# Chunk 0's first product in units of 128 tokens by four column blocks, in an attention kernel followed by a gated two-layer product

## The chip, the cores and the metric

The kernel runs on one core of a Trainium2 chip. The metric is the device time of one execution in microseconds (us). The core has a matrix engine (TensorE, PE in the profile, with its weight loads shown apart as PEld), a vector engine (VectorE, DVE), a scalar engine (ScalarE, ACT), GpSimd (POOL) and SyncE (SP). Each works through its own queue in the order in which the program issues instructions to it; semaphores hold an instruction until its inputs are there. POOL and SP also issue DMA transfers.

## The reference

```python
# q, k, v: 8 batches, 8 heads, 576 positions, 64 wide
def phi(x, c, s):                       # c, s: cosine and sine of the position
    r = np.maximum(x, 0.0)
    return np.concatenate([r * c, r * s], axis=-1)
q_p = phi(q, cos_w, sin_w); k_p = phi(k, cos_w, sin_w)
kv  = np.einsum('bhsf,bhsd->bhfd', k_p, v)
z   = np.sum(k_p, axis=2)
x   = (q_p @ kv) / (q_p @ z + 1e-6)     # per head; heads joined: 4608 tokens x 512
h   = x @ w_in                          # 512 -> 2048
g   = h * np.cos(h)
out = g @ w_out                         # 2048 -> 512
```

## The kernel before, in words

The 4608 tokens are cut into nine chunks of 512 for the two products, and into eight batches of 576 for the attention. Attention for a batch has these steps, each a small function:

- `load_q`, `load_kv`, `load_rest`: DMA loads on POOL's queue, from float32 to float16. A batch's q is kept as six parts of 96 rows.
- `scaled(b, which, i)`: one part of q or k through the map phi, two instructions (cosine and sine half), on VectorE (L143), a few of batch 0 on ScalarE (L138).
- `q_turn(b, i)`: eight TensorE transpositions of a scaled part of q (L167) into PSUM, and a copy to the tile X. For batches from 2 on, a DMA transposition on SP's queue does this.
- `spread_v`: v is copied into a tile vz, in which each row of 64 is followed by ones, so that one matmul gives kv and z. Batch 0 has no vz; there an access pattern takes 64 ones from the end of v's own tile, and the matmuls are 128 columns wide (L219) rather than 65 (L209).
- `kv_head(b, h)`: five accumulating matmuls for one head, and a copy of four heads to the tile kvz (L224).
- `num_tile(b, t)`: for a tile of 128 tokens, eight matmuls give numerator and denominator (L235), VectorE adds 1e-6 (dn, L242), takes the reciprocal (rd, L246) and multiplies (x, L255).
- `x_turn(b, t)`: four TensorE transpositions of x (L273) and a copy into XT (L281 on ScalarE, L279 on VectorE), the input of the first product.

The first product of a chunk, `m1_group`, takes one block of 128 columns of w_in at a time: four matmuls of 512 tokens (L288), the cosine on ScalarE (co, L294), the product g on VectorE (L297). Chunk 0 is done in two halves of 256 tokens, so that it can begin when two x tiles are there: 32 steps. The second product, `m2_part`, accumulates sixteen matmuls (L307) for each 128 tokens, ScalarE copies the result (ost, L314), and SP's queue stores it.

The order of everything is written out by hand (`tc.manual_schedule()`): `plan_stage0`, `plan_ahead` and `plan_tiles` put steps of attention into a table under (chunk, step) with `at(c, s, f, ...)`, and `run(c, s)` issues what stands there right behind step s of the products. Batch 0's attention comes ahead of the products and among chunk 0's first product, batch 1's among chunk 0's second product. `warm(n)` issues n matmuls on zeros.

PSUM has two pools: psA (tag att, two buffers) for attention, and psM (tags m1 and m2, two buffers each) for the products and some early attention tiles.

Of the kernel before, what the change touches and what calls it, by code (L numbers as in the profile page):

```python
# [11 lines left out]
ALU = mybir.AluOpType  # L12
# [5 lines left out]
def kernel(  # L18
# [14 lines left out]
    R = 6  # L33
# [39 lines left out]
    KB = [cpool.tile([PK, H * RUNK], F16, name=f"k{n}") for n in "ab"]  # L73
    VB = [cpool.tile([PK, H * RUNK + D], F16, name=f"v{n}") for n in "ab"]
    ID = cpool.tile([P, P], F16, name="ID")
# [72 lines left out]

    def q_turn(b, i, tag="m1"):
        s = st[b]  # L150
        if i == 0:
            s["X"] = apool.tile([P, H, S], F16, name="X", tag="X")
        if b >= 2:
            nc.sync.dma_start_transpose(
                out=s["X"][:, :, i * PR:(i + 1) * PR], in_=s["qp"][:, i],
            )
            return
        if b == 1:
            if i % 2 == 0:
                s["QT"] = psA.tile([P, 2, H, P], F16, name="QT", tag="att")  # L160
            QT = s["QT"][:, i % 2]
        elif i >= 4:
            QT = psA.tile([P, 2, H, P], F16, name="QT", tag="att")[:, 0]
        else:
            QT = psM.tile([P, H, P], F16, name="QT", tag=tag)
        for h in range(H):
            nc.tensor.matmul(  # L167
                QT[:, h, 0:PR], lhsT=s["qp"][:, i, h * F:(h + 1) * F], rhs=ID[0:PR, 0:PR],
                is_transpose=True,
            )  # L170
        if b == 1 and i % 2 == 0:
            return
        i0 = i - (b == 1)
        dst = s["X"][:, :, i0 * PR:(i + 1) * PR]
        if b == 1 and i > 1:
            nc.vector.tensor_copy(
                out=dst.rearrange("p h (a c) -> p a h c", a=2),
                in_=s["QT"][:, :, :, 0:PR],
            )
        elif b == 1:  # L180
            nc.scalar.activation(
                out=dst.rearrange("p h (a c) -> p a h c", a=2),
                in_=s["QT"][:, :, :, 0:PR], func=AF.Copy,
            )
        else:
            nc.scalar.activation(out=dst, in_=QT[:, :, 0:PR], func=AF.Copy)

    def spread_v(b, h):
        s = st[b]
        if h == 0:  # L190
            s["vz"] = apool.tile([PK, H, RK, VS], F16, name="vz", tag="vz", bufs=1)
            nc.gpsimd.memset(s["vz"][:, :, :, D:VS], 1.0)
        src = s["v16"][:, 0:H * RUNK].rearrange("p (h i d) -> p h i d", i=RK, d=D)
        dst = s["vz"][:, h:h + 2, :, 0:D]
        if b != 2:
            nc.scalar.activation(out=dst, in_=src[:, h:h + 2], func=AF.Copy)  # L196
        else:
            nc.vector.tensor_copy(out=dst, in_=src[:, h:h + 2])

    def kv_head(b, h):  # L200
        s = st[b]
        if h == 0 or (b == 0 and h == 4):
            s["KV"] = psA.tile([P, H, P], F32, name="KV", tag="att")
        if h == 0:
            s["kvz"] = apool.tile([P, H, D + 1], F16, name="kvz", tag="kvz")
        n = P if b == 0 else D + 1
        for i in range(RK):
            if b > 0:
                nc.tensor.matmul(  # L209
                    s["KV"][:, h, 0:n], lhsT=s["kp"][:, i, h * F:(h + 1) * F],  # L210
                    rhs=s["vz"][:, h, i, 0:n], start=(i == 0), stop=(i == RK - 1),
                )
                continue
            base = s["v16"][:, h * RUNK + i * D: h * RUNK + (i + 1) * D]
            vz = bass.AP(
                tensor=base.tensor, offset=base.offset,
                ap=[list(base.ap[0]), [H * RUNK - h * RUNK - i * D, 2], [1, D]],
            )
            nc.tensor.matmul(  # L219
                s["KV"][:, h], lhsT=s["kp"][:, i, h * F:(h + 1) * F], rhs=vz,  # L220
                start=(i == 0), stop=(i == RK - 1),
            )
        if h % 4 == 3:
            nc.scalar.activation(  # L224
                out=s["kvz"][:, h - 3:h + 1], in_=s["KV"][:, h - 3:h + 1, 0:D + 1],
                func=AF.Copy,
            )

    def num_tile(b, t, whole=True):
# [30 lines left out]
    def x_turn(b, t):  # L260
# [3 lines left out]
        if b >= 2:  # L264
            nc.sync.dma_start_transpose(out=XT[:, :, n0:n0 + new], in_=x[P - new:P, :])
            return
        if b == 0 and t < 2:
            XPf = psM.tile([P, 1024], F16, name="XP", tag="m1")
        else:
            XPf = psA.tile([P, 2048], F16, name="XP", tag="att")  # L270
        XP = XPf[:, 0:NCT * P].rearrange("p (i c) -> p i c", c=P)
# [10 lines left out]

    def m1_group(c, j, n0=0, n1=CH):
        if ("g", c) not in st:
            st["g", c] = gpool.tile([P, NJT, CH], F16, name="g", tag="g")
        M1 = psM.tile([P, CH], F32, name="M1", tag=("m1", "m2")[j % 2])
        for i in range(NCT):
            nc.tensor.matmul(  # L288
                M1[:, n0:n1], lhsT=w_in_sb[:, i, j * P:(j + 1) * P],
                rhs=XT[:, i, c * CH + n0:c * CH + n1],  # L290
                start=(i == 0), stop=(i == NCT - 1),
            )
        co = opool.tile([P, CH], F32, name="co", tag="co")
        nc.scalar.activation(  # L294
            out=co[:, n0:n1], in_=M1[:, n0:n1], func=AF.Sin, bias=PIH, scale=1.0,
        )
        nc.vector.tensor_tensor(  # L297
            out=st["g", c][:, j, n0:n1], in0=M1[:, n0:n1], in1=co[:, n0:n1], op=ALU.mult,
        )
# [27 lines left out]
    def at(c, s, f, *args):  # L327
        plan.setdefault((c, s), []).append((f, args))

    HS = NJT  # L330
    M2S = NJT
# [10 lines left out]
    def plan_stage0():  # L342
        at(0, 1, q_turn, 0, 4)
        at(0, 2, scaled, 0, "q", 5)
        at(0, 3, x_turn, 0, 2)
        at(0, 4, loads, 2, "kvq")
        at(0, 6, q_turn, 0, 5)
        for t, n in ((3, 9), (4, HS + 6)):
            at(0, n, num_tile, 0, t, False)
            at(0, n + 1, normalise, 0, t, 0, 1)  # L350
            at(0, n + 2, normalise, 0, t, 1, 2)
            at(0, n + 5, x_turn, 0, t)
        z = 2 * HS
        for i in range(R):
# [3 lines left out]
        for n in range(4):  # L358
            at(0, z + 1 + n, spread_v, 1, 2 * n)
        for h in range(4):  # L360
            at(0, z + 4, kv_head, 1, h)
        for i in range(2):
            at(0, z + 5, q_turn, 1, i)
        for h in range(4, H):
            at(0, z + 5, kv_head, 1, h)
        for i in range(2, R):
            at(0, z + 5 + i // 2, q_turn, 1, i)
        for n, f, t in ((7, num_tile, 0), (8, num_tile, 1), (9, x_turn, 0),
                        (10, num_tile, 2), (10, x_turn, 1), (12, num_tile, 3),
                        (13, x_turn, 2), (14, x_turn, 3), (14, num_tile, 4)):  # L370
            at(0, z + n, f, 1, t)
        at(1, 2, x_turn, 1, 4)
        for i, n in enumerate((9, 10, 11, 12, 13)):
            at(0, z + n, scaled, 2, "k", i)
        for n in range(4):
            at(0, z + 12 + n, spread_v, 2, 2 * n)
        for i, n in enumerate((-1, 1, 2, 4, 6, 8)):
# [39 lines left out]
    with tc.manual_schedule():  # L417
# [9 lines left out]
        nc.scalar.activation(out=WS, in_=PIH, func=AF.Sin)  # L427
        tiles_for(0)
        load_kv(0, "k", 0, 4)
        load_rest(0, "k")  # L430
        load_kv(0, "k", 4, 8)
        load_q(0, 0, 4)
        for h in range(0, H, 2):
            if h == 2:
                load_rest(0, "v")
            load_kv(0, "v", h, h + 2)
        nc.gpsimd.memset(st[0]["v16"][:, H * RUNK:], 1.0)
        load_w_in(0)
        load_q(0, 4, R)
        for g in range(1, 4):  # L440
# [11 lines left out]

        warm(33)
        for h0 in (0, 4):
            for i in range(RK):
                scaled(0, "k", i, h0, h0 + 4)
        for i in range(4):
            scaled(0, "q", i)
            if i < 2:
                q_turn(0, i)  # L460
        for h in range(8):
            kv_head(0, h)
        q_turn(0, 2, "m2")
        num_tile(0, 0)
        q_turn(0, 3)
        warm(1)
        num_tile(0, 1)
        warm(3)
        x_turn(0, 0)
        warm(2)  # L470
        scaled(0, "q", 4)
        x_turn(0, 1)
        num_tile(0, 2)
        for s in range(2 * HS):
            n = s // HS * (CH // 2)
            m1_group(0, s % HS, n, n + CH // 2)
            run(0, s)
        order = [(m, g) for p in (0, 2) for g in range(2) for m in (p, p + 1)]
        order += [(m, g) for m in range(NSUB) for g in range(2, 4)]
        for s, (m, g) in enumerate(order):  # L480
            m2_part(0, m, g)
            run(0, 2 * HS + s)
        for c in range(1, NCHUNK):
# [37 lines left out]
```

## Time and profile before

| | us |
|---|---|
| median of 3 runs (lowest, highest) | 300.72 (299.48, 300.94) |
| the profiled execution's own time | 299.56 |
| its span, first to last instruction | 297.8 |
| TensorE matmuls busy | 290.4 (98%) |
| VectorE busy | 190.3 (64%) |
| ScalarE busy | 158.7 (53%) |
| first matmul of the first product (L288) | 19.19 |
| first matmul of the second product (L307) that runs on without a stop | 36.71 |
| chunk 1's first product | 56.35 |

The first three rows are times of executions. The busy times are sums over one profiled execution, and the last three rows are moments in it, counted from the start of the span. A matmul's busy time is modelled and overlaps that of the next, so a high share doesn't say that TensorE never waited; the chain that ended last and the stages do.

### The profile page before, as it was taken

The numbers are of one execution on the slowest core, as the hardware profiler recorded it, in microseconds if no ns is written. First come the engines' busy times: TensorE is split into PE (matmuls) and PEld (weight loads), VectorE is DVE, ScalarE is ACT, GpSimd is POOL, SyncE is SP. The second block draws the span as 40 slices with busy tenths as digits, with TensorE's granted clock in tenths as the row PEclk, the third lists the DMA queues.
The fourth block names the chain that finished last, engine by engine and source line by source line (L and its number), as shares of the span: only waits on it lengthen the run. The fifth ranks groups of instructions, "written<-read, shape, count | busy, mean of one in ns | idle before, by whom it ended". The sixth has DMA issues, their size and how long they took to land.

```text
span 297.8 us, 5456 instructions
## 1 busy us (share of the span) xinstructions
PE 290.4 (98%) x2031; PEld 150.9 (51%) x2031; DVE 190.3 (64%) x470; ACT 158.7 (53%) x261; POOL 39.8 (13%) x65
## 2 busy tenths in 40 slices
PE   8999999999999999999999999999999999999994
PEld 3577756554544544455445544554455444444441
DVE  1668987988489666966686768677766267007600
ACT  1589952676357624762477158715771177137511
POOL 8733310005004002100210022000000000000000
PEclk9999999999999999999999999999999999999999
DMA  6999999589999996996799959996702610121022
GB/s 89 181 203 206 200 206 200 155 108 134 188 170 147 179 186 117 199 168 130 123 165 181 149 116 169 161 163 136 163 16 70 118 35 0 41 76 28 0 73 70
DMA packets 78019, 38.84 MB, mean 130 GB/s; under 512 B 48296, under 2 KB 73384, under 8 KB 77992
## 3 DMA queue, kind: packets, MB, share of 16 engines
q0 software_dynamic: 28240, 18.36, 44.1%
q1 hardware_dynamic: 49752, 20.13, 38.6%
q8 instruction: 16, 0.26, 0.4%
q14 instruction: 11, 0.09, 0.1%
HBM read 36.76 MB, written 9.44 MB: 155 GB/s over the span
## 4 chain that ended last, share of the span: by engine, by line
PE 89%; DVE 5%; DMA 3%; ACT 1%; POOL 1%; issue 1%; ACTq 0%; POOLq 0%
PE M L307 42%; PE M L288 38%; PE NP L235 3%; DVE g L297 3%; PE KV L209 3%; DMA q<-in_q_dram 3%; PE QT L167 1%; ACT co L294 1%; PE KV L219 1%; PE XP L273 1%; DVE qp L143 1%; POOL ka L108 1%; DVE x L255 0%; PE W L451 0%; POOL ka L115 0%
## 5 line engine op out<-in xcount | busy, mean ns | idle before, releaser
L297 DVE TENSOR_TENSOR g<-M,co 128x512 f16<-128x512 f32 (+1 forms) x160 | 99.9, 635 | 57.5 <-ACT co L294 57.4
L307 PE MATMUL M<-w_out_sb,g 128*128 128x512 f16 x576 | 132.3, 379 | 0.1
L288 PE MATMUL M<-XT,w_in_sb 128*128 128x512 f16 (+1 forms) x640 | 129.5, 358 | 0.6 <-DVE dn L242 0.3
L294 ACT ACTIVATE co<-M,PIH 128x512 f32<-128x512 f32 (+1 forms) x160 | 101.9, 647 | 27.5 <-PE M L288 27.0
L288 PEld LDWEIGHTS <-w_in_sb 128*128 128x128 f16 x640 | 61.3, 98 | 59.7 <-issue 0.9
L307 PEld LDWEIGHTS <-g 128*128 128x128 f16 x576 | 53.8, 98 | 58.7 <-issue 0.3
L314 ACT ACTIVATE ost<-M 128x512 f32<-128x512 f32 x36 | 21.5, 597 | 93.4 <-PE M L307 68.4
L255 DVE TENSOR_TENSOR x<-NP,rd 128x512 f16<-128x512 f32 (+1 forms) x42 | 27.9, 664 | 4.9 <-DMA XT<-x 3.6
L143 DVE TENSOR_SCALAR qp<-q,CS 96x512 f16<-96x512 f16 x94 | 28.5, 350 | 2.1 <-DMA q<-in_q_dram 1.2
L143 DVE TENSOR_SCALAR kp<-ka,CS 116x512 f16<-116x512 f16 (+1 forms) x75 | 21.6, 345 | 5.4 <-DMA ka<-in_k_dram 5.4
L235 PEld LDWEIGHTS <-X 128*128 128x128 f16 x320 | 15.3, 98 | 8.7 <-issue 0.8
L100 POOL DMA_DIRECT2D q<-in_q_dram x9 | 7.0, 779 | 90.8 <-DVE qp L143 88.2
L235 PE MATMUL NP<-kvz,X 128*128 128x65 f16 x320 | 17.0, 194 | 0.2 <-issue 0.2
L242 DVE TENSOR_SCALAR dn<-NP 128x8 f32<-128x8 f32 x40 | 6.5, 162 | 15.4 <-PE NP L235 15.2
L196 ACT ACTIVATE vz<-va 116x640 f16<-116x640 f16 x20 | 13.5, 727 | 0.0
L451 PE MATMUL W<-WU 128*128 128x512 f16 x39 | 12.0, 470 | 1.2 <-DVE PIH L426 1.2
L209 PEld LDWEIGHTS <-kp 116*128 116x128 f16 x280 | 10.7, 98 | 3.1
L209 PE MATMUL KV<-vz,kp 116*128 116x65 f16 x280 | 11.2, 193 | 0.0
L246 DVE RECIPROCAL rd<-dn 128x8 f32<-128x8 f32 x40 | 8.1, 203 | 1.4
L108 POOL DMA_DIRECT2D ka<-in_k_dram x8 | 6.5, 817 | 18.3 <-DVE kp L143 14.9
L451 PEld LDWEIGHTS <-WU 128*128 128x128 f16 x39 | 4.4, 117 | 7.2 <-issue 3.9
L224 ACT ACTIVATE kvz<-KV 128x260 f16<-128x260 f32 x16 | 6.2, 387 | 3.3 <-PE KV L209 2.3
(35 smaller groups left out, 74.5 us busy)
## 6 DMA issues: line engine op xcount, KB each, us to landing
out_dram<-ost SPq DMA_DIRECT2D x24, 192.0 KB, 2.3
q<-in_q_dram POOLq DMA_DIRECT2D x7, 576.0 KB, 7.6
ka<-in_k_dram POOLq DMA_DIRECT2D x6, 560.0 KB, 13.2
va<-in_v_dram POOLq DMA_DIRECT2D x6, 560.0 KB, 11.8
out_dram<-ost SPq DMA_DIRECT2D x24, 128.0 KB, 5.9
w_in_sb<-in_moe_w_in_dram POOLq DMA_DIRECT2D x4, 512.0 KB, 9.9
w_out_sb<-in_moe_w_out_dram POOLq DMA_DIRECT2D x4, 512.0 KB, 16.7
out_dram<-ost SPq DMA_DIRECT2D x24, 64.0 KB, 3.1
```

Source lines behind the costliest of these rows:

```text
L108: nc.gpsimd.dma_start(out=rows_of(st[b][which + "16"])[0:FULL, h0:h1], in_=full[:, h0:h1],)
L143: nc.vector.tensor_scalar(out=dst[:, h0:h1, t, :], in0=src[:, h0:h1, i, :], scalar1=0.0, scalar2=cs[:, t], op0=ALU.max, op1=ALU.mult,)
L196: nc.scalar.activation(out=dst, in_=src[:, h:h + 2], func=AF.Copy)
L209: nc.tensor.matmul(s["KV"][:, h, 0:n], lhsT=s["kp"][:, i, h * F:(h + 1) * F], rhs=s["vz"][:, h, i, 0:n], start=(i == 0), stop=(i == RK - 1),)
L235: nc.tensor.matmul(NP[:, h // 4, o:o + D + 1], lhsT=s["X"][:, h, c0:c0 + P], rhs=s["kvz"][:, h], start=True, stop=True,)
L255: nc.vector.tensor_tensor(out=x4[:, a0:a1], in0=np4[:, a0:a1, :, 0:D], in1=rd[:, a0:a1].broadcast_to((P, a1 - a0, 4, D)), op=ALU.mult,)
L288: nc.tensor.matmul(M1[:, n0:n1], lhsT=w_in_sb[:, i, j * P:(j + 1) * P], rhs=XT[:, i, c * CH + n0:c * CH + n1], start=(i == 0), stop=(i == ...
L294: nc.scalar.activation(out=co[:, n0:n1], in_=M1[:, n0:n1], func=AF.Sin, bias=PIH, scale=1.0,)
L297: nc.vector.tensor_tensor(out=st["g", c][:, j, n0:n1], in0=M1[:, n0:n1], in1=co[:, n0:n1], op=ALU.mult,)
L307: nc.tensor.matmul(M2, lhsT=st["g", c][:, j, m * P:(m + 1) * P], rhs=w_out_sb[:, j], start=(j == 0), stop=(j == NJT - 1),)
L314: nc.scalar.activation(out=ost, in_=M2, func=AF.Copy)
L451: nc.tensor.matmul(W, lhsT=WU[:, 0:P], rhs=WU, start=True, stop=True)
```

## The change

- Chunk 0's first product is done by `m1_unit(u, k_, t)`: 128 tokens (tile t) by four column blocks (group k_), 16 matmuls of 128 columns into one PSUM buffer, then one cosine and one product g of 128x512. There are 16 units, in the order written in `units`. x tile 1 is turned inside unit 0.
- Batch 0 gets a vz tile as the others have; VectorE sets the ones and spreads v in four pieces. Its matmuls are 65 columns wide. Heads 4 to 7 are copied to kvz in twos.
- The first x tile of batch 0 is made in two halves of four heads (`first_half`), each turned by itself (`first_turn`).
- The first load of q brings three parts in place of four, the second the other three. The parts 1 and 3 of batch 0 are copied to X by VectorE.
- Part 3 of q, and x tiles 2 and 3, are placed among the units; parts 3, 4 and 5 are each turned right behind their scaling. Batch 1's heads, turns and x tiles stand later in chunk 0's second product, and its v is spread by both engines.

Lines of the diff that the steps speak of:

```diff
-    def q_turn(b, i, tag="m1"):
+    def q_turn(b, i, tag="m1", evict=True):
...
-        elif i >= 4:
+        elif i >= 3:
             QT = psA.tile([P, 2, H, P], F16, name="QT", tag="att")[:, 0]
...
+    def q_evict(b, i):
...
+        if b == 0 and i in (1, 3):
+            nc.vector.tensor_copy(out=dst, in_=QT[:, :, 0:PR])
...
-        if b != 2:
+        if b > 2 or b == 1 and h < 4:
             nc.scalar.activation(out=dst, in_=src[:, h:h + 2], func=AF.Copy)
         else:
             nc.vector.tensor_copy(out=dst, in_=src[:, h:h + 2])
...
+    def first_half(a):
+        s = st[0]
+        NP = psM.tile([P, 4, P], F32, name="NP", tag="m1")
+        for h in range(4):
+            nc.tensor.matmul(
+                NP[:, h, 0:D + 1], lhsT=s["X"][:, 4 * a + h, 0:P], rhs=s["kvz"][:, 4 * a + h],
+                start=True, stop=True,
+            )
...
+    def m1_unit(u, k_, t):
+        M1 = psM.tile([P, 4, P], F32, name="M1", tag=("m1", "m2")[u % 2])
+        for j in range(4):
+            for i in range(NCT):
+                f0 = (4 * k_ + j) * P
+                nc.tensor.matmul(
+                    M1[:, j], lhsT=w_in_sb[:, i, f0:f0 + P],
+                    rhs=XT[:, i, t * P:(t + 1) * P],
+                    start=(i == 0), stop=(i == NCT - 1),
+                )
+        if u == 0:
+            x_turn(0, 1)
+        co = opool.tile([P, 4, P], F32, name="co", tag="co")
+        nc.scalar.activation(out=co, in_=M1, func=AF.Sin, bias=PIH, scale=1.0)
+        nc.vector.tensor_tensor(
+            out=g_for(0)[:, 4 * k_:4 * k_ + 4, t * P:(t + 1) * P], in0=M1, in1=co,
+            op=ALU.mult,
+        )
...
     def plan_stage0():
-        at(0, 1, q_turn, 0, 4)
+        for i in (3, 4):
+            at(0, 1, scaled, 0, "q", i)
+            at(0, 1, q_turn, 0, i)
+        at(0, 1, num_tile, 0, 2)
         at(0, 2, scaled, 0, "q", 5)
+        at(0, 2, q_turn, 0, 5)
         at(0, 3, x_turn, 0, 2)
+        at(0, 3, num_tile, 0, 3)
         at(0, 4, loads, 2, "kvq")
-        at(0, 6, q_turn, 0, 5)
-        for t, n in ((3, 9), (4, HS + 6)):
...
+        at(0, 5, x_turn, 0, 3)
+        at(0, 9, num_tile, 0, 4, False)
...
-        for n, f, t in ((7, num_tile, 0), (8, num_tile, 1), (9, x_turn, 0),
-                        (10, num_tile, 2), (10, x_turn, 1), (12, num_tile, 3),
-                        (13, x_turn, 2), (14, x_turn, 3), (14, num_tile, 4)):
+        for n, f, t in ((9, num_tile, 0), (10, num_tile, 1), (11, x_turn, 0),
+                        (12, num_tile, 2), (12, x_turn, 1), (13, num_tile, 3),
+                        (14, x_turn, 2), (14, num_tile, 4), (15, x_turn, 3)):
...
+        ones_for(0, nc.vector)
...
-        load_q(0, 0, 4)
+        load_q(0, 0, 3)
...
-        nc.gpsimd.memset(st[0]["v16"][:, H * RUNK:], 1.0)
         load_w_in(0)
-        load_q(0, 4, R)
+        load_q(0, 3, R)
...
-        warm(33)
+        warm(31)
...
-        for i in range(4):
+        for i in range(2):
             scaled(0, "q", i)
-            if i < 2:
-                q_turn(0, i)
-        for h in range(8):
+            q_turn(0, i, evict=(i == 0))
+        for h in range(H):
+            if h == 4:
+                q_evict(0, 1)
+                scaled(0, "q", 2)
+                q_turn(0, 2, "m2", evict=False)
+            if h % 2 == 0:
+                spread_v(0, h)
+            if h == 6:
+                first_half(0)
             kv_head(0, h)
-        q_turn(0, 2, "m2")
...
+        q_evict(0, 2)
+        first_turn(0)
+        first_half(1)
+        warm(2)
+        first_turn(1)
         num_tile(0, 1)
...
-        for s in range(2 * HS):
-            n = s // HS * (CH // 2)
-            m1_group(0, s % HS, n, n + CH // 2)
+        units = [(0, 0), (0, 1), (1, 0), (1, 1), (0, 2), (1, 2), (0, 3), (1, 3)]
+        units += [(g, t) for g in (2, 3) for t in range(NSUB)]
+        for s, (g, t) in enumerate(units):
+            m1_unit(s, g, t)
             run(0, s)
```

## The prediction

> **What bounds the kernel now.** I read the page first, then busy time by stage, then the chain that ended last, then the timeline of the first 40 us. All times are us of the profiled execution, from the span's start.
>
> ```profile
> PE 290.4 (98%) x2031; PEld 150.9 (51%) x2031; DVE 190.3 (64%) x470; ACT 158.7 (53%) x261; POOL 39.8 (13%) x65
> L307 PE MATMUL M<-w_out_sb,g 128*128 128x512 f16 x576 | 132.3, 379 | 0.1
> ```
>
> TensorE is nearly always busy, but matmul busy time overlaps itself, so the page alone doesn't say where it waits. The stages do:
>
> ```profile
> core 0: us, PE busy (x) PEld busy (x) DVE busy (x) ACT busy (x) POOL busy (x), PEclk, DMA share, GB/s
> 19.19:36.71 17.52, 16.68 (x172) 14.19 (x173) 14.69 (x43) 16.33 (x38) 5.16 (x7) 1.00 1.29 204
> 36.71:56.35 19.64, 19.60 (x208) 11.76 (x208) 16.34 (x53) 8.96 (x15) 1.75 (x4) 1.00 1.19 198
> ```
>
> The first row is chunk 0's first product (L288 with L294 and L297): ScalarE is busy for 16.33 of 17.52. The second is chunk 0's second product with batch 1's attention between, where TensorE never rests. The chain says the same:
>
> ```profile
> 19.19 0.61 PE M L288 x4
> ...
> 30.18 0.42 DVE g L297
> 30.62 0.42 DVE g L297
> 31.06 0.42 DVE g L297
> ...
> 36.71 4.49 PE M L307 x20
> 41.20 0.64 PE KV L209 x20
> 41.84 0.87 PE M L307 x4
> ```
>
> Until 36.71 the chain runs over VectorE and ScalarE (one g per 0.44); from there it is TensorE to the end, four matmuls of 512 columns in 0.87. So the end moves by as much as the moment at which TensorE gets into unbroken second-product work, plus what is lost among batch 1's steps. The diff changes nothing behind these.
>
> The third thing to see is how TensorE treats a transposition of q whose scaled part is not there yet:
>
> ```profile
> 16.93 0.60 POOL L115 DMA_DIRECT2D kb<-in_k_dram  x1 [1.13 <-DMA w_in_sb<-in_moe_w_in_dram]
> 18.00 0.83 POOL L108 DMA_DIRECT2D vb<-in_v_dram  x1 [0.47 <-DMA q<-in_q_dram]
> 18.23 1.32 ACT L138 ACTIVATE qp<-q,CS 96x512 f16<-96x512 f16 x2
> 20.06 0.51 PE L167 MATMUL QT<-ID,qp 96*128 96x96 f16 x8
> 20.50 0.60 POOL L115 DMA_DIRECT2D vb<-in_v_dram  x1 [1.66 <-DMA w_in_sb<-in_moe_w_in_dram]
> 22.17 0.60 DVE L143 TENSOR_SCALAR qp<-q,CS 96x512 f16<-96x512 f16 x2
> 22.83 0.51 PE L167 MATMUL QT<-ID,qp 96*128 96x96 f16 x8
> ```
>
> Part 4 of q is scaled from 18.23 to 19.55 and turned at 20.06; part 5 is scaled from 22.17 to 22.77 and turned at 22.83, four steps behind in the program. No L288 matmul of a later step passes a turn; matmuls run in program order.
>
> **The change, up to the first product.** The first q load has 3 parts, 288 KB for 384, in rows of 384 bytes for 512, still 768 rows. By bytes it saves a quarter of the 2.35 between the second k landing (VectorE resumes at 8.63) and q's (3.44 and 7.52 in the chain), 0.6; by rows, nothing. POOL's issues, each released by a landing, give the rate of the second q load with 256-byte rows: 16.93 to 18.00 for 192 KB, 179 KB/us, against 205 KB/us for the next w_in piece (18.00 to 20.50 for 512 KB). Short rows cost little, so I take 0.45, and v and w_in group 0 behind it as much; the second q load then lands where it did. The Trainium skill's page "DMA: Bandwidth & Descriptors" (Specifications) speaks against the cut: under 512 bytes a transfer does a read-modify-write and leaves line rate. Were it to double the load, q would land at 12.4 and the sum would be 1.9 worse; the 179 KB/us says no.
>
> Then, by rows: two parts of q scaled (four at 0.345) to 11.9; two v copies of 116x640 on VectorE (0.32 each, L198) to 12.5; heads 0 to 3 (20 matmuls, 0.64, L209) to 12.85; on VectorE q1's copy (128x768, 0.55 between 0.42 at 512 and 0.96 at 1536), q2's scaling 0.65, two more v copies 0.6: 14.2. The first x half: dn 0.17, rd 0.20, x 0.42 (128x256, L255) from 14.7 to 15.5, turned and copied by ScalarE behind X of q2 (0.80); the second half follows the first turn on TensorE, x done at 16.9, copied by VectorE at 17.5. So the first product starts at 17.4, 1.8 ahead of 19.19. The memset of va on POOL (0.22) and the new ones' memset on VectorE lie in idle time. Nothing moves past SP's queue.
>
> **The change, in the first product.** 128 matmuls of 256 columns become 256 of 128. The row for 128 columns is L219: 40 in 2.23, 0.056 each with their weight loads; so 14.3 against 13.9 (0.1085 each). ScalarE's 32 steps of 0.44 (14.1) become 16 of 0.69 (11.0), VectorE's the same: with 0.89 of TensorE per unit, TensorE would be the bound. With the turns and x tiles of batch 0 in this stage (three QT of 0.34, three NP of 0.26, four XP of 0.22, the fifth x tile in two steps) TensorE has 17.0 of work of its own, so it could be done at 34.4.
>
> But the order puts part 3 of q here as well, and each turn directly behind its scaling, which stands behind the g of its own unit. VectorE's order is: copy of x tile 1, g of unit 0, g of unit 1, q3, copy of q3, x tile 2, g of unit 2, q5. TensorE's is: unit 1, turn of q3, turn of q4, NP of tile 2, unit 2, turn of q5, unit 3. Walking it, with 0.2 from TensorE's last matmul to the reader:
> - Unit 0 17.3 to 18.3. x tile 1 is ready at 18.6, turned, copied by VectorE (0.42) at 19.5; unit 1 19.5 to 20.4. Waits 1.0.
> - Turn of q3: cos of unit 1 (0.69) 20.6 to 21.3, its g (0.60 to the next) to 21.9, q3 scaled (two, 0.67) to 22.6. **Wait 2.2.** Turns of q3 and q4 to 23.3; VectorE copies q3 to 23.75; **wait 0.45**; NP of tile 2 to 24.0; unit 2 to 24.9. Queued behind the waiting turn are units 2 and 3, whose w_in groups had landed by 16.93 and 20.50.
> - Turn of q5: ScalarE first copies q4 (0.80), then cos 25.1 to 25.8, g to 26.45, q5 to 27.1. **Wait 2.2.** Unit 3 27.5 to 28.4.
> - Unit 4 needs x tile 2: XP at 28.6, ScalarE does q5's copy, cos of unit 3, then the copy (0.60), 29.85. **Wait 1.0.** Units 4 and 5 and XP of tile 3 to 31.9.
> - Unit 6 needs tile 3: cos of unit 5, then its copy, 33.1. **Wait 1.3.** Units 6 to 15 run on: 42.7.
>
> 17.3, plus 17.0 of work, plus 8.4 of waits. M2's second accumulator needs the last unit's PSUM buffer, free at its g's end, 44.3; 20 matmuls run on from there, 24 counted from 43.5. Before, 36.71. Walked with the same rows, the kernel before gets there at 37.4, 0.7 late. So 6.1 to 6.8 later; I take 6.1, like with like.
>
> **Batch 1's part.** Its v is spread by ScalarE (two, 1.37) and VectorE (two, 0.6); heads, turns and x tiles come two steps later. Up to the 13th step TensorE has cover (its 0.86 per step). Then x tile 3's turn comes after the last second-product matmul, and chunk 1's first product needs it: ScalarE's ost copy (0.60) and XT copy (0.60) lie open, 1.15; NP of tile 4 waits 0.5 for a PSUM buffer that x tile 2's copy holds. Before, 55.15's XP had 1.1 of work behind it and about 0.2 was lost. So +1.4; bounds 0.5 (copies change places) and 1.6.
>
> **Sum.** +6.1 +1.4 = +7.5 on the profiled execution's 299.56 (span 297.8 and 1.76 around it): 307.0. The median of the three runs is 300.72, 1.2 above, so a median may fall nearer 308.
>
> **Rivals.**
> - *Faster.* The turns don't stop TensorE: it does 17.0 of work from 17.4 plus the 1.0 for x tile 1, and second-product work starts at 36.0 or, with nothing lost, 35.0: 1.7 ahead. Less batch 1's 1.4, 299.3; without that, 297.9. It decides on whether VectorE has q3 scaled before unit 1 ends at 20.4. For it: q's second load lands before 18.0, and VectorE is idle from 20.0 to 21.3. Against it: q3 stands behind g of unit 1, which can't start before 21.3. Chance 0.03.
> - *Half the waits*: cos and g overlap more than the rows show, or ScalarE's copies come sooner: 4.2 of waits for 8.4, 303. Chance 0.07.
> - *TensorE's clock falls in the gaps.* In this trace the first warm-up loads are 0.43 apart until 6.71, then 18 in 3.79, 0.21 apart: a fresh clock is half, for 5.5. The granted clock is 1.00 in every stage, whose gaps stay under 0.7. From 20.4 to 27.2 TensorE would work 1.8 of 6.8. If that takes the clock, units 3 to 6 run at half for up to 5.5 and lose 2.75: 310. Chance 0.12. The Trainium skill ("TensorE: Matmul & The Clock Gate", Part 1) wants a whole idle window of about 3.4 us for the fall; by that rule gaps of 2.2 don't do it and the sum stays, and no run here shows such gaps.
> - *No effect*: gain at the start and waits cancel; needs waits of 2, 300 to 301. Chance 0.04.
>
> **How the numbers follow.** Forecast 0.74, 305 to 308.5, its bounds being 0 to 0.6 at the load, 6.1 to 6.8, 0.5 to 1.6, and the 1.2 between the profile and the median. Half the waits 0.07, clock 0.12, no effect 0.04, faster 0.03. The range 304.3 to 310.0 takes in the forecast and the lower half of the clock case, and leaves out 0.20. About 0.5% (1.5 us) is what a measurement can tell from no change; faster by that 0.03, within 0.04, slower 0.93.
>
> **What would show it.** In the profile after: turns of q (L167) at about 22.6 and 27.2 that wait for VectorE's qp, each ending about 2.2 of TensorE idle; first-product units 0.89 apart only from unit 6; second product from about 43; chunk 1's first product from about 64 for 56.35, then equal stages. It is wrong if unit 2 starts before 22, or if units run faster or slower than 0.056 per matmul.

## The result, and the profile after

The changed kernel takes 310.99 us (median of 5, 308.72 to 311.52) against 300.07 for the kernel before (median of 5, 298.96 to 300.94): a ratio of 1.0355, 95% interval 1.0306 to 1.0404. It is slower, as forecast, and by more: 310.99 lies above the 307.0 of the forecast and above the range's end of 310.0. The profiled execution took 311.52, its span is 309.4, and its granted clock averages 0.989, against 0.999 before.

The page says where to look: the clock row, which is 9 in nearly every slice, falls to 7 and 8 in the fourth and fifth.

```profile
PE   8757899989999998999999999999999999999994
...
PEclk9997899999999999999999999999999999999999
```

The two stages of the prediction, first product and then second product with batch 1, in the same columns as before:

```profile
17.73:46.02 28.29, 22.00 (x330) 20.14 (x327) 16.35 (x35) 15.00 (x24) 7.55 (x11) 0.88 1.29 204
46.02:67.12 21.10, 19.11 (x206) 11.39 (x204) 16.36 (x53) 8.11 (x14) 0.17 (x1) 1.00 0.55 99
```

The first product starts 1.46 earlier (17.73 for 19.19) and its stage takes 28.29 for 17.52, of which TensorE is busy for 22.00, at a mean granted clock of 0.88. The second stage is 1.46 longer (21.10 for 19.64), at full clock. The moments 46.02 and 67.12 are the second product, counted so that the four matmuls done before its last stop are subtracted (46.88 less 0.86), and chunk 1's first product.

The chain that ended last, in order of time, shows what the end of the first stage hangs on (start, length, work):

```profile
21.84 0.69 DVE g L333
22.54 0.53 DVE qp L143 x2
...
23.11 1.30 PE QT L167 x16
...
25.03 1.72 PE M L324 x16
...
26.78 0.70 ACT co L332
...
27.50 0.69 DVE g L333
28.19 0.53 DVE qp L143 x2
...
28.76 0.51 PE QT L167 x8
29.28 0.91 PE M L324 x16
```

Cosine, g, scaling of q, turn: twice, as walked. But the same unit of 16 matmuls takes 1.72 at 25.03 and 0.91 at 29.28. The granted clock over stretches of 3.41, laid on the moments at which it changes (columns as in the stages):

```profile
19.92:23.34 3.42, 1.28 (x22) 1.11 (x22) 1.87 (x5) 1.90 (x3) 0.79 (x2) 1.00 1.24 207
23.34:26.75 3.41, 3.39 (x39) 2.90 (x36) 1.62 (x4) 0.81 (x1) 1.36 (x2) 0.50 1.24 207
26.75:30.16 3.41, 1.40 (x27) 1.40 (x28) 1.21 (x3) 1.50 (x2) 0.75 (x1) 1.00 1.26 204
30.16:33.58 3.42, 2.91 (x34) 2.80 (x32) 1.66 (x4) 1.42 (x3) 0.84 (x1) 0.50 1.36 200
33.58:36.99 3.41, 2.37 (x43) 2.25 (x41) 1.38 (x2) 1.86 (x4) 1.42 (x2) 1.00 1.36 200
```

A stretch with a wait for a turn of q in it, TensorE 1.28 or 1.40 busy out of 3.41, is followed by a stretch at half clock. That happens twice. The 1.72, 1.9 times the 0.91, lies wholly within the first stretch at half clock.

### The profile page after: what moved, and what is told of

Its sections match the earlier page's. It is cut to its first block, busy times and chain, and to the rows that moved or that the text cites. A ratio compares the mean times of both kernels' runs of the same rounds, so it can differ in the third digit from the quotient of the medians.

```text
span 309.4 us, 5661 instructions
## 1 busy us (share of the span) xinstructions
PE 291.9 (94%) x2153; PEld 153.9 (50%) x2153; DVE 192.2 (62%) x466; ACT 153.4 (50%) x242; POOL 39.9 (13%) x64
## 4 chain that ended last, share of the span: by engine, by line
PE 84%; DMA 7%; DVE 4%; ACT 2%; issue 1%; POOL 1%; ACTq 0%; POOLq 0%
PE M L360 37%; PE M L341 34%; PE M L324 5%; DMA X<-qp 5%; PE NP L269 3%; PE KV L218 3%; DMA va<-in_v_dram 2%; PE QT L167 1%; ACT co L332 1%; DVE qp L143 1%; DVE x L289 1%; DVE g L333 1%; ACT XT L312 1%; POOL ka L108 1%; PE XP L304 0%
## 5 line engine op out<-in xcount | busy, mean ns | idle before, releaser
L350 DVE TENSOR_TENSOR g<-M,co 128x512 f16<-128x512 f32 x128 | 87.2, 690 | 54.7 <-ACT co L347 54.6
L341 PE MATMUL M<-XT,w_in_sb 128*128 128x512 f16 x512 | 113.9, 379 | 1.0 <-ACT XT L312 1.0
L347 ACT ACTIVATE co<-M,PIH 128x512 f32<-128x512 f32 x128 | 88.0, 688 | 27.3 <-PE M L341 27.0
L341 PEld LDWEIGHTS <-w_in_sb 128*128 128x128 f16 x512 | 49.2, 98 | 58.3 <-issue 1.1
L289 DVE TENSOR_TENSOR x<-NP,rd 128x512 f16<-128x512 f32 (+1 forms) x40 | 27.1, 678 | 5.1 <-DMA XT<-x 3.8
L324 PE MATMUL M<-XT,w_in_sb 128*128 128x128 f16 x256 | 17.6, 232 | 2.1 <-ACT XT L312 1.5
L324 PEld LDWEIGHTS <-w_in_sb 128*128 128x128 f16 x256 | 16.5, 104 | 2.6 <-issue 2.4
L333 DVE TENSOR_TENSOR g<-M,co 128x512 f16<-128x512 f32 x16 | 11.0, 690 | 9.9 <-ACT co L332 9.6
L332 ACT ACTIVATE co<-M,PIH 128x512 f32<-128x512 f32 x16 | 11.0, 687 | 10.7 <-PE M L324 10.4
L218 PEld LDWEIGHTS <-kp 116*128 116x128 f16 x320 | 12.4, 98 | 3.8 <-issue 0.3
L218 PE MATMUL KV<-vz,kp 116*128 116x65 f16 x320 | 13.0, 194 | 0.3 <-DVE dn L238 0.2
L167 PE MATMUL QT<-ID,qp 96*128 96x96 f16 x96 | 5.9, 216 | 5.8 <-DVE qp L143 5.8
```

The lines of the kernel that those rows point to most:

```text
L218: nc.tensor.matmul(s["KV"][:, at_, 0:D + 1], lhsT=s["kp"][:, i, h * F:(h + 1) * F], rhs=s["vz"][:, h, i, 0:D + 1], start=(i == 0), stop=(i ...
L289: nc.vector.tensor_tensor(out=x4[:, a0:a1], in0=np4[:, a0:a1, :, 0:D], in1=rd[:, a0:a1].broadcast_to((P, a1 - a0, 4, D)), op=ALU.mult,)
L324: nc.tensor.matmul(M1[:, j], lhsT=w_in_sb[:, i, f0:f0 + P], rhs=XT[:, i, t * P:(t + 1) * P], start=(i == 0), stop=(i == NCT - 1),)
L332: nc.scalar.activation(out=co, in_=M1, func=AF.Sin, bias=PIH, scale=1.0)
L333: nc.vector.tensor_tensor(out=g_for(0)[:, 4 * k_:4 * k_ + 4, t * P:(t + 1) * P], in0=M1, in1=co, op=ALU.mult,)
L341: nc.tensor.matmul(M1, lhsT=w_in_sb[:, i, j * P:(j + 1) * P], rhs=XT[:, i, c * CH:(c + 1) * CH], start=(i == 0), stop=(i == NCT - 1),)
```

## The experiments

All start from the changed kernel unless another base is named. The second product is counted as above. The profiled executions don't all start alike: the first product stands at 17.73 in the changed kernel, at 17.19 to 17.73 in other versions whose program is the same up to there, so moments of two profiles are compared with that shift taken off.

### Fill the two waits, leave everything else

TensorE gets transpositions with nothing to do ahead of the two waiting turns; the turns stay where they are, and so do their waits for VectorE.

In `q_turn`, ahead of the turn:

```diff
+        for n in range(FILL if b == 0 and i in (3, 5) else 0):
+            nc.tensor.matmul(
+                QT[:, n % H, 0:PR], lhsT=s["qp"][:, 2, (n % H) * F:(n % H + 1) * F],
+                rhs=ID[0:PR, 0:PR], is_transpose=True,
+            )
```

FILL = 40:

> The change, with 40 more transpositions of part 2 of q (96 columns, about 0.0425 us each, 1.7 us together) put on TensorE ahead of the turns of parts 3 and 5, into the same PSUM tile, whose contents the real turns then overwrite. They fill each wait of 2.0 us and change no other instruction. (A) If the gate's half clock is what the profile shows to cost about 3 us, the granted clock stays at 1.00 and the time falls by about 3 us to 308. If only one of the two windows is held, 309.5. (B) If the half clock lay in waits and cost nothing, or if the gate falls for another reason than TensorE's idle time, 311 and the clock falls as before. (C) If the transpositions don't end in time they delay the real turns and the time rises by up to 0.5 us over A.

Measured: 308.09 (median of 4, 307.80 to 308.45), ratio 1.0271 (1.0245 to 1.0297), mean clock 1.000 in three executions and 0.994 in one. The stretches that were 1.28 and 1.40 busy, and the one between them, in this kernel:

```profile
19.74:23.15 3.41, 3.09 (x65) 2.94 (x65) 1.71 (x4) 1.91 (x3) 0.60 (x1) 1.00 1.24 206
23.15:26.56 3.41, 3.10 (x71) 2.95 (x68) 2.16 (x5) 1.50 (x2) 1.18 (x2) 1.00 1.24 207
26.56:29.98 3.42, 2.29 (x46) 2.06 (x44) 1.20 (x4) 1.98 (x3) 1.12 (x2) 1.00 1.26 206
```

And its chain:

```profile
24.37 0.91 PE M L330 x16
...
27.34 0.51 PE QT L173 x8
27.85 0.91 PE M L330 x16
...
44.44 4.48 PE M L366 x20
...
64.69 2.75 PE M L347 x12
```

Eighty useless instructions on TensorE make the kernel 2.9 faster (310.99 to 308.09). Unit 2 takes 0.91 again, and the second product counts from 43.58 (44.44 less 0.86) for 46.02. Of these 2.44, 0.34 is no effect of the fills: the first waiting turn, before any fall of the clock, already stands at 22.77 in this execution for 23.11 in the changed kernel's. So the fall of the clock is worth 2.10 there, and from the changed kernel's start the second product would count from 43.92 at full clock. The rest of the loss, 36.71 to 43.92, is there without any fall: the waits themselves.

FILL = 8 and 16:

> As the kernel with 40 transpositions ahead of the turns of parts 3 and 5, but with 8 (0.34 us). What tells is how far TensorE must be busy for the clock to hold. In the profiles so far the gate changes on a grid of 3.41 us; windows of the first product with TensorE busy for 0.29 to 0.41 of the time were followed by one at half clock, windows from 0.44 on were not. (A) A threshold on the busy share of a whole window: the filling lifts 0.35 and 0.41 to about 0.45 and 0.5, and the clock holds in most executions, about 308.5 us; where the grid lies as in the kernel with batch 1's old steps (0.29 and 0.30 unfilled), it still falls, 310 to 311. (B) The gate wants one unbroken idle stretch: that is still 1.7 us, nearly the 2.0 of the change, and the clock falls in all executions, 311.

> As before, with 16 transpositions (0.68 us) ahead of each of the two turns: window shares of about 0.5 and more wherever the grid lies. (A) Threshold on a window's share: clock 1.00 in all executions, 308.1 us as with 40. (B) Unbroken idle stretch (1.35 us left): in between, 308 to 311.

Measured: 310.30 with 8 (median of 4, 308.07 to 311.30; ratio 1.0350, 1.0297 to 1.0404; mean clocks 0.980 to 0.994) and 308.84 with 16 (308.53 to 309.54; 1.0294, 1.0256 to 1.0331; clocks 0.989, 0.999, 0.989, 1.000). With 16 two executions of four keep the clock and two don't; with 8, none keeps it throughout. The profiled execution with 16 lost it behind a stretch half busy. The one with 8 lost it ahead of the waits, behind a stretch 0.62 busy, and held it behind one half busy (second fence):

```profile
21.37:24.78 3.41, 1.75 (x37) 1.56 (x36) 2.11 (x6) 2.12 (x4) 0.78 (x1) 1.00 1.24 206
24.78:28.19 3.41, 2.67 (x33) 2.45 (x31) 1.93 (x5) 0.69 (x1) 0.78 (x1) 0.50 1.26 211
```

```profile
11.94:15.35 3.41, 2.13 (x49) 1.69 (x45) 2.94 (x9) 0.92 (x4) 2.85 (x4) 1.00 1.32 202
15.35:18.77 3.42, 3.34 (x31) 2.44 (x32) 2.09 (x7) 1.01 (x3) 1.44 (x2) 0.50 1.34 204
...
25.59:29.01 3.42, 1.74 (x36) 1.59 (x33) 1.33 (x4) 1.48 (x3) 1.18 (x2) 1.00 1.25 205
29.01:32.42 3.41, 2.51 (x46) 2.30 (x44) 2.14 (x5) 2.06 (x4) 0.84 (x1) 1.00 1.36 199
```

Neither theory came out whole. One threshold on the share (A) wanted full clock in every execution with 16, and two of four lost it; one unbroken idle stretch (B) wanted the fall in every execution with 8, and the profiled one held the clock through both waits. Nor does the length of the gap sort them: TensorE stood for 1.34 in the stretch that lost the clock with 16, and for 1.68 in the one that held it with 8. Over the stretches read in the first product and ahead of it, full-clock stretches in which TensorE was 0.37 to 0.42 busy were followed by half clock each time (five, in three kernels); from 0.49 to 0.62 some were and some not; above that none was. (The expectation's 0.29 and 0.30 are 0.39 and 0.36 in this view.)

### The same turns, scaled one unit earlier

```diff
         for i in (3, 4):
-            at(0, 1, scaled, 0, "q", i)
+            at(0, 0, scaled, 0, "q", i)
             at(0, 1, q_turn, 0, i)
-        at(0, 2, scaled, 0, "q", 5)
+        at(0, 1, scaled, 0, "q", 5)
         at(0, 2, q_turn, 0, 5)
```

> The change, with parts 3, 4 and 5 of q scaled one unit earlier than they are turned. Three theories. (A) Order and clock: TensorE stands before the two turns because their scaled parts sit behind the g of the unit before (2.0 us each in the trace), and the clock gate then takes half the clock for two windows of 3.41 us, some 3 us of work. Moving the scaling ahead takes about 2.4 us of waits (the copies of q3 and q4 still stand behind g of unit 1, so part of the wait moves to the x tile) and holds the clock at 1.00 through the first product: about 305.5 us for 311.0, first unbroken second-product matmul near 40.6 us. (A') The same, but the gate still falls for one window: 307. (B) Finer units: the cost lies in the 256 matmuls of 128 columns and 16 hand-overs to ScalarE and VectorE, and the waits only hide it: 309 or more, clock as in the change.

Measured: 306.49 (median of 4, 305.56 to 307.91), ratio 1.0224 (1.0178 to 1.0269), mean clocks 0.994 to 0.998. The timeline of TensorE (start, busy, and in brackets the idle time before it with its releaser):

```profile
21.15 0.85 PE L167 MATMUL QT<-ID,qp 96*128 96x96 f16 x16
23.05 0.43 PE L269 MATMUL NP<-kvz,X 128*128 128x65 f16 x8 [1.05 <-DVE X L181]
...
25.22 0.51 PE L167 MATMUL QT<-ID,qp 96*128 96x96 f16 x8 [0.85 <-DVE qp L143]
```

The first turn shows no wait for scaling any more (2.02 in the changed kernel, below), but 1.05 of it comes back one step on, where x tile 2 waits for the copy of q's part 3. The second is down to 0.85. The second product counts from 41.47 (42.33 less 0.86): with the first product at 17.73 in both profiles, 4.55 earlier than in the changed kernel. Of this the clock is 2.10, by the fills, and the waits 2.45. The position of the scaling among VectorE's instructions, one unit of the schedule, decides how long TensorE's queue stands, and through that whether the clock falls.

### Batch 1 as before

Batch 1's plan and its v spread by ScalarE alone are put back; batch 0 stays as changed.

```diff
-        if b > 2 or b == 1 and h < 4:
+        if b != 2 and b > 0:
...
-            at(0, z + 3, spread_v, 1, 2 * n)
+            at(0, z + 1 + n, spread_v, 1, 2 * n)
... (batch 1's heads, turns, x tiles and batch 2's spreading as in the kernel before)
```

> The change, with batch 1's steps among chunk 0's second product as in the kernel before (v spread by ScalarE one step at a time, heads, turns and x tiles two steps earlier). (A) The stage from the first unbroken second-product matmul to chunk 1's first product takes 19.7 us for 21.1 in the change, and the time falls by about 1.4 us to 309.6. (B) If the later steps cost nothing of themselves and the stage was long only because chunk 0 came late, it stays at 21.1 and the time at 311.

Measured: 310.34 (median of 4, 309.21 to 311.12), ratio 1.0343 (1.0304 to 1.0381), mean clocks 0.977 to 0.981. The stage did what was expected of it: from 46.33 (47.19 less 0.86) to 65.95 in TensorE's timeline, 19.62, where the changed kernel takes 21.10 and the kernel before 19.64. The time hardly moved, because three stretches ran at half clock in place of two:

```profile
19.09:22.51 3.42, 1.34 (x20) 1.04 (x18) 1.83 (x4) 1.98 (x4) 0.60 (x1) 1.00 1.24 206
22.51:25.92 3.41, 2.94 (x34) 2.73 (x35) 1.71 (x6) 1.19 (x2) 1.18 (x2) 0.50 1.24 208
25.92:29.33 3.41, 1.22 (x13) 0.96 (x12) 1.69 (x4) 0.69 (x1) 1.12 (x2) 0.50 1.25 204
29.33:32.75 3.42, 3.03 (x34) 2.91 (x32) 0.50 (x1) 1.98 (x3) 0.84 (x1) 0.50 1.37 199
```

The second gap here lies within a half-clock stretch, and the clock doesn't come back after it. Nothing in the edit touches these 14 us; in this profile the grid of 3.41 lies elsewhere against the gaps (its edge at 22.51, in the changed kernel's at 23.34, with the first waiting turn at 22.97 and 23.11). That this is why the third stretch was lost is likely and not shown: all four executions here have mean clocks of 0.977 to 0.981, the changed kernel's five 0.983 to 0.991. A comparison of times alone would have said that batch 1's part costs nothing.

### No wait for q, and batch 1 as before

The units' order lets TensorE do all four column groups of x tiles 0 and 1 first; scaling stands a unit or more ahead of its turn, and turns and tiles stand later. Batch 1 is as in the experiment above.

```diff
-        for i in (3, 4):
-            at(0, 1, scaled, 0, "q", i)
-            at(0, 1, q_turn, 0, i)
-        at(0, 1, num_tile, 0, 2)
+        at(0, 0, scaled, 0, "q", 3)
+        at(0, 0, scaled, 0, "q", 4)
+        at(0, 1, q_turn, 0, 3)
+        at(0, 2, q_turn, 0, 4)
         at(0, 2, scaled, 0, "q", 5)
-        at(0, 2, q_turn, 0, 5)
-        at(0, 3, x_turn, 0, 2)
-        at(0, 3, num_tile, 0, 3)
+        at(0, 3, num_tile, 0, 2)
+        at(0, 4, q_turn, 0, 5)
...
-        at(0, 5, x_turn, 0, 3)
+        at(0, 6, x_turn, 0, 2)
+        at(0, 6, num_tile, 0, 3)
+        at(0, 8, x_turn, 0, 3)
...
+        units = [(0, 0), (0, 1), (1, 0), (1, 1), (2, 0), (2, 1), (3, 0), (3, 1),
+                 (0, 2), (1, 2), (0, 3), (1, 3), (2, 2), (2, 3), (3, 2), (3, 3)]
```

(In chunk 0 the second product's accumulator also alternates between the two PSUM tags.)

> The units of the change with the waits taken out of TensorE's order: parts 3 and 4 of q scaled behind unit 0, turned behind units 1 and 2, part 5 scaled behind unit 2 and turned behind unit 4; the units run over all four column groups of tokens 0 to 255 first, so that x tiles 2 and 3 are needed eight units later; batch 1's steps as in the kernel before; chunk 0's second product takes its PSUM buffers by turns from both tags. (A) The clock stays at 1.00, second-product work runs on from about 36.3 us (before: 36.7), and the time is that of the kernel before or up to 1 us less: 299.2 to 300.2. (B) If the finer units themselves are slow (over 0.92 us of TensorE per unit in unbroken stretches, or the clock falls in them), 303 or more.

Measured: 300.22 (median of 10, 299.03 to 302.03), ratio 1.0016 (0.9993 to 1.0039): the whole loss is gone, and nothing is gained. The edit changes the order of the units, the places of scaling, turns and tiles, batch 1's steps and the accumulators at once; it doesn't tell their shares apart. Mean clocks 0.997 to 0.999 in seven executions, 0.981 to 0.989 in the three slowest, 301.19 to 302.03. Busy time over the first product, and the chain:

```profile
17.50:37.00 19.50, 18.28 (x319) 17.12 (x319) 15.07 (x34) 14.00 (x22) 6.00 (x8) 1.00 1.29 204
```

```profile
12.22 13.86 DMA w_in_sb<-in_moe_w_in_dram
...
26.13 1.08 PE M L324 x16
...
37.02 4.32 PE M L360 x20
```

And TensorE's timeline:

```profile
36.85 4.48 PE L360 MATMUL M<-w_out_sb,g 128*128 128x512 f16 x20
```

TensorE is busy for 18.28 of 19.50. The first unit starts at 17.19, 2.0 ahead of the kernel before, and the second product at 36.85, 0.1 behind it (the chain has 37.02, since it counts a step from the end of the one before). The early start is spent on TensorE's own work: this stage holds 18.28 of it where the kernel before, from 19.19 to 36.71, had 16.68.

### Units or halves, in that order

Base: the kernel of the last experiment. Chunk 0's first product in 32 steps of 256 tokens by one column block, as before, x tiles 2 and 3 turned a unit earlier, the rest as there.

```diff
+    def m1_half(j, n0):
...
-        for s, (g, t) in enumerate(units):
-            m1_unit(s, g, t)
-            run(0, s)
+        x_turn(0, 1)
+        for s in range(2 * NJT):
+            m1_half(s % NJT, s // NJT * (CH // 2))
+            if s % 2:
+                run(0, s // 2)
```

> The kernel with late turns, but with chunk 0's first product in the 32 half steps of 256 tokens by one column block that the kernel before has, in place of 16 units; the attention steps keep their order among them, except that x tile 2 and 3 are turned one unit earlier, since the second half needs both. It isolates the form of the units. (A) The units are worth about 2 us where nothing waits: halves can't start before x tile 1 is there (19.5 for 17.2), ScalarE sets their pace (0.44 a step), and the second half waits for x tile 3; second product from about 38.7, 302 us. (B) The units are worth nothing: 300.2 as the kernel with late turns. The clock stays at 1.00 in both.

Measured: 302.73 (median of 10, 300.70 to 304.58), ratio 1.0097 (1.0067 to 1.0126), mean clocks 0.981 to 0.996. Against the 300.22 of its base the units are 2.5 better. In the chains of the profiled executions the second product stands at 38.04 for 37.02; this execution, the quickest of the ten, also turned its first x tile 0.41 earlier (16.40 for 16.81), so 1.4 of the 2.5 is there at full clock. The rest goes with the lower clocks, and which of its gaps does that isn't settled. In this order, then, the units are a gain.

### Warm matmuls in the remaining waits

Base: the same kernel. Ten matmuls on zeros (the expectation says nine) are put into the waits ahead of and in unit 0.

```diff
         if u == 0:
+            st["warm"](1)
             x_turn(0, 1)
+            st["warm"](3)
...
             scaled(0, "q", i)
+            warm(2 - i)
             q_turn(0, i, evict=(i == 0))
...
                 scaled(0, "q", 2)
+                warm(2)
                 q_turn(0, 2, "m2", evict=False)
...
         q_evict(0, 2)
+        warm(1)
         first_turn(0)
```

> The kernel with late turns, with nine more matmuls on zeros (512 columns, 0.216 us each) put where TensorE waits in the start: two and one ahead of the first turns, two ahead of the turn of part 2, one ahead of the first x half's turn, one ahead of and three behind the turn of x tile 1. They go where waits of 0.2 to 0.7 us stand in that kernel's trace. (A) The clock holds in every execution (that kernel's mean clock was 0.981 to 0.989 in three of ten, and those took 301.2 to 302.0), so the spread shrinks to 299.0 to 300.4 and the median falls to about 299.9, no different from the kernel before. (B) If the falls there have another cause, three in ten still take over 301. (C) If they delay the start, 0.2 to 0.5 us more in all executions.

Measured: 300.08 (median of 12, 299.32 to 300.77) against 300.13 for the kernel before, ratio 0.9989 (0.9965 to 1.0014), mean clocks 0.996 to 1.000 in all twelve. None of the twelve took over 301 at a lower clock, as three of its base's ten did; with so few, in two sessions, chance isn't excluded, and the kernel before itself took 302.73 and 303.23 in two of its 17 executions here, at a mean clock of 0.994. It is level with the kernel before; no version here beats it.

### Four parts of q in the first load

```diff
-        load_q(0, 0, 3)
+        load_q(0, 0, 4)
-        load_q(0, 3, R)
+        load_q(0, 4, R)
```

> The change with the first load of q bringing four parts and the second two, as in the kernel before; nothing else. (A) The load goes by its bytes: q lands about 0.5 us later after the second k load than in the change (2.3 for some 1.8), and with it the first scaled part. (B) It goes by its rows, 768 in both: no difference. The time stays within 0.6 us of the change in either case, apart from how many windows the clock falls in.

One execution, 313.41, mean clock 0.977: half clock in four stretches, so its time says nothing about the load. The landings do. POOL issues the second load of q when k's second piece has landed, and the next piece of w_in when q's first load has; in the changed kernel, with three parts:

```profile
9.42 0.79 POOL L100 DMA_DIRECT2D q<-in_q_dram  x1 [1.19 <-DMA ka<-in_k_dram]
10.96 2.25 POOL L121 DMA_DIRECT2D w_in_sb<-in_moe_w_in_dram  x3 [0.75 <-DMA q<-in_q_dram]
```

From the one to the other four parts take 2.12 here and 2.34 in the kernel before. Three parts take 1.54 in the changed kernel, and 1.35 to 2.23 in the seven profiles that show both waits. Mostly less, then, and nothing like a doubling from the shorter rows; but the two ranges touch, and how much three parts save these runs don't fix.

## Why the prediction was wrong, by its own steps

The direction, the waits and batch 1's part held; the time did not. The step that failed is the clock: the sum has its fall in the waits at nothing and leaves it to a rival with a chance of 0.12, and it fell twice. With TensorE kept busy in the waits the same kernel took 308.09, within the forecast's 305 to 308.5. A second step was mis-sized: the 6.1, which at full clock was 7.2. In the profiled pair the forecast's +7.5 became +11.96:

| | predicted | measured |
|---|---|---|
| second product later, at full clock | 6.1 | 7.21 (43.92 by the run with fills, 36.71 before) |
| fall of the clock, at the second product | 0 (rival: 2.75, chance 0.12) | 2.10 (46.02 less 43.92) |
| batch 1's part | 1.4 | 1.46 |
| later in the kernel | 0 | 0.83 |
| outside the span | 0 | 0.36 (2.12 for 1.76) |

**The clock.** The rival named the place, the price (2.75 for 2.10) and nearly the time (310, measured 310.99), and got 0.12. The clock fell behind stretches of 3.41 in which TensorE was busy for 1.28 and 1.40, with gaps of 2.0. What held the chance down was a rule. The Trainium skill's page "TensorE: Matmul & The Clock Gate" (Part 1) has the clock fall after a whole idle window of about 3.4 us. By that rule waits of 2.0 leave it up, and this trace disagrees; the length agrees (each half-clock stretch in the first products of these profiles is 3.41 or a multiple). The rival's own working had the evidence: "from 20.4 to 27.2 TensorE would work 1.8 of 6.8" is a share of 0.26, and the kernel before had no stage with a share near that, so its trace couldn't vouch for the clock either way. The fills show the cause: the waits unchanged, only TensorE occupied in them, and the clock comes back, and with it 2.10 in the profiles and 2.9 in the medians. With the case at a half, the range would have had to reach through it, to the forecast's upper 308.5 plus 2.75, 311.3.

**The 6.1.** The walk said 43.5 against 36.71, 6.8; I subtracted the 0.7 by which the same walk missed the kernel before. Its moments were good: in the run with fills, whose first product stood at 17.4 as walked, the second product counts from 43.58, and chunk 1 from 64.69, where the prediction's terms give 64.5. So there was no error to subtract here. Why the walk missed the kernel before by 0.7 isn't shown. The other 0.3 of the 7.2 is the later start of the changed kernel's profiled execution.

**The waits.** The turns start at 23.11 and 28.76, predicted 22.6 and 27.2 (with the fills 22.77 and 27.34). The profile gives each wait as 2.02. The prediction's 2.2 counts from the unit's start plus 16 times 0.056; by that count the first is 2.2 as well (20.03 and 0.9 to 23.11). The waits that the prediction names add up to 8.15, where its sum takes 8.4:

```profile
23.11 1.29 PE L167 MATMUL QT<-ID,qp 96*128 96x96 f16 x16 [2.02 <-DVE qp L143]
...
28.76 0.51 PE L167 MATMUL QT<-ID,qp 96*128 96x96 f16 x8 [2.02 <-DVE qp L143]
...
35.65 3.73 PE L324 MATMUL M<-XT,w_in_sb 128*128 128x128 f16 x64 [1.04 <-ACT XT L312]
```

The last line shows the wait for x tile 3 as well (1.04, and 1.2 by the prediction's count; predicted 1.3), and units that run on from there at 0.056 per matmul (64 in 3.57 of the chain), as sized. The units' readers came out as sized too, 0.69 for each cosine and each g.

**The start.** First product at 17.73, predicted 17.4; 1.46 ahead, predicted 1.8. The start differs by up to 0.5 between profiles of the same steps (17.19 to 17.73), so neither number is finer than that. The load's 0.45 lies within the spread of the landings, which doesn't fix it. The Trainium skill's page "DMA: Bandwidth & Descriptors" (Specifications) has a read-modify-write under 512 bytes. No doubling shows in these 384-byte rows (1.35 to 2.23 for 2.12 and 2.34).

**Batch 1's part**, 1.4, was right to 0.1, and the run with batch 1 as before shows that it is that part: 19.62 for 21.10. Its waits stand where they were walked, in the changed kernel:

```profile
64.60 0.43 PE L269 MATMUL NP<-kvz,X 128*128 128x65 f16 x8 [0.36 <-DVE x L289]
...
67.12 2.75 PE L341 MATMUL M<-XT,w_in_sb 128*128 128x512 f16 x12 [1.00 <-ACT XT L312]
```

They are 0.36 for 0.5 and 1.00 for 1.15; the first is put down to VectorE's product x, not to a copy of x tile 2.

**Later in the kernel** 0.83 was lost, which the prediction had at nothing. The chain has it at a DMA transposition of q that a TensorE step of batch 3 waits for:

```profile
97.70 8.01 PE M L341 x38
105.71 13.96 DMA X<-qp
119.67 0.90 issue
120.57 0.42 PE NP L269 x8
```

With the 40 fills, chunk 1's first product stands at 64.69 of 305.8, which leaves 241.1, as before (241.45); in the changed kernel it leaves 242.3. So this loss isn't in every execution; why the transposition is late in that execution is open.

**What the earlier start is worth** without the waits, the order without them shows: it starts at 17.19, and TensorE is busy for 18.43 up to 36.85, so 35.6 at best, 1.1 ahead of 36.71. The waits that order still has, one of 0.23 for the last piece of w_in before 26.13, take that and a little more.

## What to carry to other kernels

Where an engine works through its queue in order, an instruction that needs another engine's work should stand at least one full turn of the pipeline behind that work; here one unit of distance was worth 2.45 us of waiting and, with the clock, 4.55. Count the share of time in which TensorE is busy over stretches of about 3.4 us as well as the length of gaps: in these traces stretches up to 0.42 busy cost half clock in the next one each time, and stretches from 0.49 to 0.62 in some executions, which shows as a spread of times. Fills that do nothing can hold the clock while the order is mended, and a term is best judged by its own stage, since the clock can hide it in the total.

## What the runs showed of the hardware

Two gaps of 2.0 each, with work between, took the clock: the stretches of 3.41 with them in were 1.28 and 1.40 busy. The half-clock stretches ahead of and in the first product are 3.41 long or two or three times that, and their edges lie at other moments in each profile (23.34 and 22.51 in the two shown). One kernel (16 fills) lost the clock in two executions and kept it in two; that the place of the edges decides it is likely, but the moments of the others aren't on record. What brings the clock back isn't settled: a half-clock stretch in which TensorE was mostly idle (1.22 of 3.41) was followed by another, but so was one with 2.94 busy in the same run, while behind 2.91 and 3.39 in the changed kernel the clock was full again. Transpositions count as work for it (the 40 fills held it), and so do matmuls on zeros (in the kernel before, with nothing else on TensorE, their weight loads go from 0.43 to 0.21 apart at 6.71).
